# M's stage of a fused attention and expert kernel, issued behind the experts with conversions between its pieces

## The chip, the cores and the metric

The kernel runs on one core of one Trainium2 chip. The metric is the device time of one execution in microseconds (us), the median of several runs. Engines are called TensorE (PE in the profile), VectorE (DVE), ScalarE (ACT), GpSimd (POOL) and SyncE (SP, which issues the DMAs).

## What is computed

Three parts follow one another. Block-causal attention over 8 batches, 8 heads, 576 positions of 64; a soft mixture of 8 experts with 4 slots each over the 4608 tokens of 512; and a last layer of 2048 hidden units whose activation is `s * relu(h)^2 + b`.

```python
def _moe_ref(x, phi, w1, w2):
    ...
    slot_input = d.T @ x
    ...
    for e in range(E):
        h = np.maximum(slot_input[e] @ w1[e], 0.0)
        slot_out[e] = h @ w2[e]
    slot_out = slot_out.reshape(n_slots, D)
    c = logits - logits.max(1, keepdims=True)
    c = np.exp(c)
    c /= c.sum(1, keepdims=True) + 1e-09
    return (c @ slot_out).astype(np.float32)

def _moe2_ref(x, w_in, w_out, s, b):
    h = x @ w_in
    r = np.maximum(h, 0.0)
    g = s * (r * r) + b
    return (g @ w_out).astype(np.float32)
```

`w_in` and `w_out` arrive as 64-bit floats, viewed as pairs of 32-bit integers.

## The kernel before, in words

Attention and routing take the first 430 us and are not touched. Then come three stages.

**Experts (lines 801 to 866).** The weights arrive in 32 pieces of 1 MB: sixteen `w1`, then sixteen `w2`. TensorE works them off with `expert1` and `expert2`, the second layer's sum growing in the PSUM tile `so`. Between the two layers stands `mid`, with ScalarE's copy `hs`. After each piece one call of `convert` issues the next step of the conversions, of which two (`CMOST`) are under way at any time.

**Conversions (`from_f64`, lines 611 to 631, `split_wo` and `conv_in`).** The 16 pieces of `w_in` (`wi`, 8) and `w_out` (`wo`, 8) are put together from the halves of the 64-bit floats: on VectorE L619, L620, L625, L627, on ScalarE L622, L623, a product L706 or L745 on VectorE. A `wo` piece then goes on: ScalarE sums its absolute values (`power`, L710, into `wsum`), VectorE and ScalarE make a power of two of each sum (`power2`, L715, L717, `wpow`), ScalarE writes the high half in 16 bits (`high`, L725, tile `wo_0s` for pieces 0 and 1, `wo_2s` for 2 and 3, and so on) and VectorE the low half (`low`, L730). Each step of a piece is a `yield`, and one call of `convert` takes one step of each active piece. The order of the instructions on each engine is that of the calls in the program. What the expert loop has not issued, the loop of L865 issues behind it.

**M's stage (lines 885 to 976).** M is the product of the expert outputs with w_in: 32 slots by 2048 columns. `slot_rows` copies the sum `so` to `sos` (L894), adds its four row groups on TensorE (L897) and copies that to `soT`. `ctrans` transposes the combine weights of the first group (`ct`). `slots(i)`, eight pieces of 256 columns, makes a product (`m`), a copy `part`, a second product with `J4` (`n`), a sum of absolute values (L914, into `msum`) and a copy into `mf`. Two scales follow: that of M from `msum` (L931 to L939), and that of the output from the maxima of the transposed `mf` (L951 to L975). Each has a product on TensorE that spreads a maximum over all partitions, `gp`. `parts` writes M's high part on ScalarE (L942) and its low part, in rows 64 to 127, on VectorE (L943), in `mst`: first 512 columns, at the end the other 1536.

**Output blocks (lines 980 to 1051).** Twelve groups of three token tiles by 16 blocks of 128 hidden units, 192 blocks. A block is `stage_h` (a product `h`, ScalarE's `r`), `stage_g` (VectorE's `g`), `stage_r` (ScalarE's `rh`, VectorE's `rl`) and `stage_o` (nine products `o` of 512 columns with the halves `hl[f]` of w_out), which is issued `LAG` = 4 blocks behind its `h`. `at(t, ...)` collects these calls with a time number, and they are issued in that order.

Of the kernel before, what the change touches and what calls it, by code (L numbers as in the profile page):

```python
# [40 lines left out]
def fused_kernel(  # L41
# [615 lines left out]
    P = {}  # L657
# [6 lines left out]
    ready, todo, active = set(), [], []  # L664

    toload = list(wseq[NPRE:])
    home = {wseq[i]: wpre[i] for i in range(NPRE)}
# [33 lines left out]
    def split_wo(i):  # L701
# [99 lines left out]
    with tc.manual_schedule():  # L801
# [55 lines left out]
        for kind, i in [x for x in wseq if x[0] in ("w1", "w2")]:  # L857
# [27 lines left out]
    with tc.manual_schedule():  # L885

        pm = ph3.enter_context(tc.tile_pool(name="pm", bufs=3, space=PSUM, reuse_waits="tile"))
        mdone = set()
# [29 lines left out]
        msum = e1.tile([128, 12], F32, name="msum")  # L918
        sb_abs = e1.tile([128, 2], F32, name="sb_abs")
        ACT.activation(out=sb_abs[:, 0:1], in_=s_sb, func=AF.Abs)  # L920
        ACT.activation(out=sb_abs[:, 1:2], in_=b_sb, func=AF.Abs)
# [9 lines left out]
        DVE.tensor_reduce(out=msum[:, 8:9], in_=msum[:, 0:8], axis=AX, op=ALU.add)  # L931
        gp = pm.tile([128, 512], F32, tag="n", name="n")
        PE.matmul(gp[:, 0:128], msum[:, 8:9].to_broadcast([128, 128]), idF, start=True, stop=True)
        DVE.tensor_reduce(out=msum[:, 9:10], in_=gp[:, 0:128], axis=AX, op=ALU.max)
        for n, x in ((10, 0x7F800000), (11, 0)):
            DVE.tensor_scalar(out=msum[:, n:n + 1].bitcast(I32), in0=msum[:, 9:10].bitcast(I32), scalar1=0x7F800000, scalar2=x,
                              op0=ALU.bitwise_and, op1=ALU.bitwise_xor)
        ACT.mul(msum[:, 10:11], msum[:, 10:11], 2.0 ** 13)
        ACT.mul(msum[:, 11:12], msum[:, 11:12], 2.0 ** -28)  # L939

        def parts(x0, x1):
            ACT.activation(out=mst[:, x0:x1], in_=mf[:, x0:x1], func=AF.Copy, scale=msum[:, 10:11])  # L942
            DVE.scalar_tensor_tensor(out=mst[64:128, x0:x1], in0=mf[64:128, x0:x1], scalar=msum[64:128, 10:11],  # L943
                                     in1=mst[64:128, x0:x1], op0=ALU.mult, op1=ALU.subtract)
            mdone.update(range(x0 // 256, x1 // 256))

        parts(0, 512)


        mt = pm.tile([128, 512], F32, tag="m", name="m")  # L950
        for f in range(16):  # L951
            PE.transpose(mt[:, 32 * f:32 * f + 32], mf[0:32, 128 * f:128 * f + 128], idF[0:32, 0:32])

        def small(name, n=16):
            return e1.tile([128, n], F32, name=name)

        mm, bound, gpow, sk, bk, rs_, mu = (small(n) for n in ("mmax", "bound", "gpow", "sk", "bk", "rscale", "mu"))
        DVE.tensor_reduce(out=mm, in_=mt.rearrange("p (f n) -> p f n", n=32), axis=AX, op=ALU.max)
# [12 lines left out]
        DVE.tensor_scalar(out=sk, in0=rs_, scalar1=s_sb, scalar2=1.0, op0=ALU.mult, op1=ALU.mult)
        DVE.tensor_scalar(out=bk, in0=rs_, scalar1=b_sb, scalar2=1.0, op0=ALU.mult, op1=ALU.mult)
        DVE.tensor_scalar(out=mu[:, 3:4].bitcast(I32), in0=mu[:, 1:2].bitcast(I32), scalar1=0x7F800000, scalar2=None,
                          op0=ALU.bitwise_and)
        DVE.tensor_scalar(out=mu[:, 3:4], in0=mu[:, 3:4], scalar1=2.0 ** -28, scalar2=None, op0=ALU.mult)  # L975
        parts(512, 2048)
    ph3.close()
    ps_h = ctx.enter_context(tc.tile_pool(name="ps_h", bufs=2, space=PSUM, reuse_waits="tile"))
    ps_o = ctx.enter_context(tc.tile_pool(name="ps_o", bufs=2, space=PSUM, reuse_waits="tile"))
    with tc.manual_schedule():  # L980
        rr_ = {}

        def stage_h(g, f):
            assert f // 2 in mdone
# [33 lines left out]
        def stage_e(g):  # L1018
            for i in range(3):
                ob = e3.tile([128, 512], F32, tag="ob", name="ob")  # L1020
                if i == 1:
                    DVE.tensor_scalar(out=ob, in0=ops[g][i], scalar1=mu[:, 3:4], scalar2=1.0, op0=ALU.mult, op1=ALU.mult)
                else:
                    ACT.activation(out=ob, in_=ops[g][i], func=AF.Copy, scale=mu[:, 3:4])
# [10 lines left out]
        def step(gen):  # L1035
            next(gen, None)

        for i in range(1, 6):
            for j in range(4):
                at(16 * (2 * i - 1) - 5 + 2 * j + 0.3, step, combs[i])  # L1040
        for n, (g, f) in enumerate(seq):
# [39 lines left out]
```

## Time and profile before

| | |
|---|---|
| median of 3 runs | 983.55 us (982.73 to 985.5) |
| profiled execution | 982.77 us |
| its span in the trace | 981.1 us |
| TensorE products | 879.0 us busy (90%) |
| VectorE | 703.6 us (72%) |
| ScalarE | 604.1 us (62%) |
| GpSimd | 286.5 us (29%) |
| data moved | 91.73 MB, 94 GB/s over the span |

Busy shares are means over stages with different limits. What the change touches lies between about 430 and 590 us of the span, so the rows further down are taken there. In a timeline, the bracket behind a row is the engine's idle time before it and what ended that; a count such as x8 for four products in 32 bits counts two passes of each.

### The profile page before, as it was taken

The page shows a single profiled execution, that of the slowest core. Times are in us where ns is not written, and L with a number is a line of the kernel's source. Part 1 is how long each engine was busy: PE and PEld are TensorE (multiplying, and loading weights), DVE is VectorE, ACT ScalarE, POOL GpSimd, SP SyncE. Part 2 cuts the span into 40 slices and gives each one's busy share as a digit, 9 for nine tenths or more (in the row PEclk, how much of TensorE's full clock was granted, in tenths as well). Part 3 has the DMA queues.
Part 4 walks back from the last instruction along what each step waited for, and adds up shares of the span by engine and source line. Part 5 has one row for each costly group of instructions (what it writes and reads, how often), then busy time and mean ns, then how long its engine had stood idle before and what let it go on. Part 6 is the DMA issues. An engine that isn't in the chain of part 4 may idle for free.

```text
span 981.1 us, 20487 instructions
## 1 busy us (share of the span) xinstructions
PE 879.0 (90%) x8052; PEld 515.1 (53%) x8052; DVE 703.6 (72%) x1269; ACT 604.1 (62%) x1040; POOL 286.5 (29%) x224
## 2 busy tenths in 40 slices
PE   3899989988999988876785699999999999999998
PEld 2677767767777767761110334444444444444443
DVE  5798979888899879848889566565555565565553
ACT  2677767777677767753377655555555555565553
POOL 6576756665566646652000000000000000000000
PEclk9999999999999999987999789999999999999999
DMA  4544544444434434075995000001000100010001
GB/s 113 130 91 118 129 109 101 102 120 115 110 81 123 123 106 112 15 302 217 410 400 214 1 1 33 11 23 33 33 1 32 33 32 2 33 33 1 33 33 32
DMA packets 150927, 91.73 MB, mean 94 GB/s; under 512 B 127472, under 2 KB 127792, under 8 KB 150832
## 3 DMA queue, kind: packets, MB, share of 16 engines
q1 hardware_dynamic: 150832, 90.44, 30.7%
q8 instruction: 63, 1.03, 0.4%
q14 instruction: 32, 0.26, 0.1%
HBM read 80.81 MB, written 9.44 MB: 92 GB/s over the span
## 4 chain that ended last, share of the span: by engine, by line
PE 58%; DVE 21%; ACT 11%; DMA 4%; issue 3%; POOL 3%; SPq 0%; DVEq 0%; POOLq 0%; ACTq 0%
PE o L1015 13%; PE o L1014 13%; PE o L1016 13%; DVE vl L356 5%; PE s L378 4%; DVE mm L292 4%; ACT pc L383 4%; PE h L986 3%; ACT ph L255 3%; PE tp L268 2%; DMA w<-in_moe_w_dram 2%; PE s L303 2%; DVE me L292 2%; PE pv L416 1%; DVE kql L262 1%
## 5 line engine op out<-in xcount | busy, mean ns | idle before, releaser
L262 POOL TENSOR_TENSOR pl<-pc,ph 128x896 f16<-128x896 f32 (+1 forms) x128 | 232.4, 1817 | 150.0 <-ACT ph L255 82.6
L994 DVE SCALAR_TENSOR_TENSOR g<-r,sk 128x384 f32<-128x384 f32 x192 | 119.4, 622 | 128.2 <-ACT r L988 126.7
L988 ACT ACTIVATE r<-h,msum 128x384 f32<-128x384 f32 x192 | 111.4, 581 | 156.4 <-PE h L986 155.3
L383 ACT ACTIVATE pc<-s 128x896 f32<-128x896 f32 (+1 forms) x128 | 110.6, 864 | 75.1 <-PE s L378 48.0
L1002 DVE SCALAR_TENSOR_TENSOR rl<-g,bk,rh 128x384 f16<-128x384 f32 x192 | 117.9, 614 | 8.0 <-ACT rh L1000 6.7
L1000 ACT ACTIVATE rh<-g,bk 128x384 f16<-128x384 f32 x192 | 116.5, 607 | 2.2 <-DVE g L994 2.2
L255 ACT CAST ph<-pc 128x896 f16<-128x896 f32 (+1 forms) x128 | 113.4, 886 | 4.1
L292 DVE TENSOR_REDUCE mm<-s 128x2 f32<-128x1024 f32 (+3 forms) x128 | 101.8, 817 | 7.3 <-PE s L303 7.1
L766 POOL TENSOR_TENSOR c<-lgs,mc 128x192 f32<-128x192 f32 x6 | 3.0, 508 | 345.6 <-DVE mc L764 345.6
L416 PE MATMUL pv<-vh,ph 128*128 128x65 f16 x960 | 102.5, 196 | 1.2 <-DVE xt L432 1.0
L418 PE MATMUL pv<-vh,pl 128*128 128x65 f16 x960 | 101.0, 194 | 1.3 <-POOL pl L262 1.3
L417 PE MATMUL pv<-vl,ph 128*128 128x64 f16 x960 | 101.4, 193 | 0.0
L416 PEld LDWEIGHTS <-ph 128*128 128x128 f16 x960 | 86.6, 98 | 23.0 <-issue 6.3
L1016 PEld LDWEIGHTS <-rl 128*128 128x128 f16 x576 | 56.4, 98 | 68.7 <-DVE rl L1002 0.7
L1014 PEld LDWEIGHTS <-rh 128*128 128x128 f16 x576 | 56.5, 98 | 66.6 <-issue 0.3
L418 PEld LDWEIGHTS <-pl 128*128 128x128 f16 x960 | 88.7, 98 | 1.6 <-POOL pl L262 1.5
L417 PEld LDWEIGHTS <-ph 128*128 128x128 f16 x960 | 88.6, 99 | 0.0
L1015 PEld LDWEIGHTS <-rh 128*128 128x128 f16 x576 | 56.5, 98 | 58.3 <-issue 0.6
L262 DVE TENSOR_TENSOR kql<-tp,kq 128x512 fp32r<-128x512 f32 (+1 forms) x96 | 57.5, 599 | 29.2 <-ACT kq L284 28.2
L268 PE MATMUL tp<-idF,rqk 128*128 128x128 f32 x320 | 57.9, 298 | 22.0 <-DVE kql L262 9.6
L303 PE MATMUL s<-kq 64*128 64x64 f32 (+4 forms) x384 | 55.3, 336 | 20.6 <-DVE me L292 14.6
L378 PE MATMUL s<-kq 64*128 64x128 f32 (+3 forms) x384 | 70.4, 363 | 0.8
(236 smaller groups left out, 1967.7 us busy)
## 6 DMA issues: line engine op xcount, KB each, us to landing
w<-in_moe_w_dram SPq DMA_DIRECT2D x44, 512.0 KB
w2h<-in_moe_w_dram SPq DMA_DIRECT2D x20, 512.0 KB
rqk<-in_k_dram SPq DMA_DIRECT2D x64, 128.0 KB
rqk<-in_q_dram SPq DMA_DIRECT2D x64, 128.0 KB
rv<-in_v_dram SPq DMA_DIRECT2D x64, 128.0 KB
wi<-in_moe_w_in_dram SPq DMA_DIRECT2D x8, 1024.0 KB
wo<-in_moe_w_out_dram SPq DMA_DIRECT2D x8, 1024.0 KB
out_dram<-ob SPq DMA_DIRECT2D x32, 256.0 KB
```

The lines of the kernel that those rows point to most:

```text
L255: ACT.copy(o, i)
L262: eng.tensor_tensor(out=o, in0=i, in1=h, op=ALU.subtract)
L292: DVE.tensor_reduce(out=o, in_=i, axis=AX, op=ALU.max)
L383: ACT.activation(out=pc[:, :, 0:w], in_=st.pop(("ps", p, c))[:, :, 0:w], func=AF.Exp, scale=scale)
L416: PE.matmul(o, a, vh[:, 2 * sl + h, 0:65], start=(c == 0 and n == 0), stop=False)
L417: PE.matmul(o[:, 0:64], a, vl[:, 2 * sl + h, :], start=False, stop=False)
L418: PE.matmul(o, l, vh[:, 2 * sl + h, 0:65], start=False, stop=(c == 3 and n == len(UNIT[c]) - 1))
L994: DVE.scalar_tensor_tensor(out=g0, in0=r, scalar=sk[:, f:f + 1], in1=r, op0=ALU.mult, op1=ALU.mult)
L1002: DVE.scalar_tensor_tensor(out=rl, in0=g0, scalar=bk[:, f:f + 1], in1=rh, op0=ALU.add, op1=ALU.subtract)
L1014: PE.matmul(o, rh[:, 128 * i:128 * i + 128], hl[f][0], start=(f == 0), stop=False)
L1015: PE.matmul(o, rh[:, 128 * i:128 * i + 128], hl[f][1], start=False, stop=False)
L1016: PE.matmul(o, rl[:, 128 * i:128 * i + 128], hl[f][0], start=False, stop=(f == 15))
```

## The change

- The second loop of conversions behind the experts is gone. `slots` yields twice, and the loop over it calls `convert` after each of its first ten rounds, then until all eight `power2` are issued (`summed`). What remains of the conversions is called in the first eight output blocks. The pool of the conversions' tiles outlives the experts for that.
- The sum of absolute values of M (L914, `msum`) is replaced. Each slot's columns of `mf` are transposed (into `mt`, in a bank of its own) as soon as they are copied; `extremes` takes maxima and minima of these, and both scales come from one round: one tile `top` of two columns, two products `gp`, one reduction, and the powers `inv`, `fm`, `fo`.
- All copies `part` and the copy `soT` are ScalarE's, the copies `mf` VectorE's but for the last.
- M's high and low parts are separate calls. Before the output blocks stand 512 columns of the high and 256 of the low part; the others are issued in blocks 0 to 11.
- The lag between `h` and `o` begins at 2 blocks and grows to 4 over the first eight.

```diff
     P["cs"] = later(ctx, "csp", 1).tile([128, NT, 64], F16, name="cs")
     e2 = later(ctx, "e2", 2)
-    P["cv"] = later(ph2, "cv", 2)
+    P["cv"] = later(ctx, "cv", 2)
...
             ACT.mul(wpow[:, 2 * i:2 * i + 2], wpow[:, 2 * i:2 * i + 2], 2.0 ** 13)
+
+            summed.add(i)
...
             convert(CMOST)
-        while todo or active:
-            convert(CMOST)
     ph2.close()
...
-            DVE.tensor_copy(soT, sop[:, 0:128].rearrange("p (c n) -> p c n", c=4))
+            ACT.copy(soT, sop[:, 0:128].rearrange("p (c n) -> p c n", c=4))
...
-            (DVE.tensor_copy if i % 2 else ACT.copy)(part, ps)
+            ACT.copy(part, ps)
             yield
             ps = pm.tile([128, 512], F32, tag="n", name="n")[:, 0:256]
             PE.matmul(ps, J4.rearrange("p a n -> p (a n)"), part, start=True, stop=True)
-
-            ACT.activation(out=part, in_=ps, func=AF.Abs, bias=eps, accum_out=msum[:, i:i + 1])
-            (ACT.copy if i % 2 else DVE.tensor_copy)(mf[:, 256 * i:256 * (i + 1)], ps)
+            (DVE.tensor_copy if i < 7 else ACT.copy)(mf[:, 256 * i:256 * (i + 1)], ps)
+            yield
+            for f in (2 * i, 2 * i + 1):
+                PE.transpose(mt[:, 32 * f:32 * f + 32], mf[0:32, 128 * f:128 * f + 128], idF[0:32, 0:32])
...
+        def extremes(f0, f1):
+
+            x = mt[:, 32 * f0:32 * f1].rearrange("p (f n) -> p f n", n=32)
+            DVE.tensor_reduce(out=mm[:, f0:f1], in_=x, axis=AX, op=ALU.max)
+            DVE.tensor_reduce(out=mn[:, f0:f1], in_=x, axis=AX, op=ALU.min)
+
         gens = [slots(i) for i in range(8)]
-        for i in range(10):
-            if i < 8:
-                next(gens[i])
-            if i >= 2:
-                next(gens[i - 2], None)
...
+        for i in range(11):
+            for j in (i, i - 2, i - 3):
+                if 0 <= j < 8:
+                    next(gens[j], None)
+            if i < 10:
+                convert(CMOST)
+        while len(summed) < 8:
+            convert(CMOST)
...
+        extremes(0, 16)
+
+
+        DVE.scalar_tensor_tensor(out=mn, in0=mn, scalar=-1.0, in1=mm, op0=ALU.mult, op1=ALU.max)
+        DVE.tensor_reduce(out=top[:, 0:1], in_=mn, axis=AX, op=ALU.max)
...
+        DVE.tensor_reduce(out=top[:, 1:2], in_=bound, axis=AX, op=ALU.max)
         gp = pm.tile([128, 512], F32, tag="n", name="n")
-        PE.matmul(gp[:, 0:128], mu[:, 0:1].to_broadcast([128, 128]), idF, start=True, stop=True)
...
+        for n in range(2):
+            PE.matmul(gp[:, 128 * n:128 * n + 128], top[:, n:n + 1].to_broadcast([128, 128]), idF, start=True, stop=True)
+        DVE.tensor_reduce(out=top, in_=gp[:, 0:256].rearrange("p (a n) -> p a n", a=2), axis=AX, op=ALU.max)
...
+        part_hi(0, 256)
...
+        part_lo(0, 256)
...
+        part_hi(256, 512)
...
+        at(0.9, part_lo, 256, 512)
+        for x in range(512, 2048, 512):
+            at(x / 128 - 2.6, part_hi, x, x + 512)
+            at(x / 128 - 1.8, part_lo, x, x + 256)
+            at(x / 128 - 0.8, part_lo, x + 256, x + 512)
+
+        for n in range(8):
+            at(n + 1.3, convert, CMOST)
...
-            at(n + LAG + .05, stage_o, g, f)
+            lag = min(LAG, 2 + n / 4) + .05
+            at(n + lag, stage_o, g, f)
```

Line numbers of the changed kernel lie a few higher: `high` is L727 there (L725 before), `low` L732, the copy `sos` L895, `soT` L899, `part` L910, `mf` L914, M's high part L971, `r` L997, `rh` L1009.

**ScalarE around the end of the experts.** In the order of the kernel before, behind the sums (L710), the powers (L717) and the high part (L725) of piece wo_2; the rows of two such rounds, down to the copy `sos`:

```order
L725 ACTIVATE wo_2s<-cvf,wpow 128x512 x2
L710 ACTIVATE cve,wsum<-cvf,eps 128x512 x2
L717 ACTIVATE wpow<-wpow 128x2
L725 ACTIVATE wo_2s<-cvf,wpow 128x512 x2
L622 ACTIVATE cvf<-wo_8667 128x1024
L623 ACTIVATE cve<-cve,m_103 128x1024
...
L717 ACTIVATE wpow<-wpow 128x2
L725 ACTIVATE wo_6s<-cvf,wpow 128x512 x2
L894 COPY sos<-so 128x512
L710 ACTIVATE cve,wsum<-cvf,eps 128x512 x2
```

and in the changed kernel, from the same high part of wo_2 (here L727):

```order
L727 ACTIVATE wo_2s<-cvf,wpow 128x512 x2
L895 COPY sos<-so 128x512
L899 COPY soT<-m 128x128
L641 COPY ct<-n 64x384
L910 COPY part<-m 128x256
L710 ACTIVATE cve,wsum<-cvf,eps 128x512 x2
L910 COPY part<-m 128x256
L717 ACTIVATE wpow<-wpow 128x2
L910 COPY part<-m 128x256
L727 ACTIVATE wo_2s<-cvf,wpow 128x512 x2
L622 ACTIVATE cvf<-wo_8667 128x1024
```

Before, `sos` stood behind the high part of wo_6 (the last but one of the eight pieces); now it stands behind that of wo_2, and the sums of wo_3 and all later conversions are behind it.

**VectorE at the same place in the changed kernel**, behind the last product (L706) of piece wo_3:

```order
L706 TENSOR_TENSOR cvf<-cvf,cve 128x1024
L642 COPY ct<-n 64x384
L732 SCALAR_TENSOR_TENSOR wo_2s<-cvf,wpow,wo_2s 128x512 x2
L715 TENSOR_SCALAR wpow<-wsum 128x2
L914 COPY mf<-n 128x256
L619 TENSOR_SCALAR cve<-wo_8667 128x1024
L620 TENSOR_SCALAR cvm<-wo_8667 128x1024
L914 COPY mf<-n 128x256
L732 SCALAR_TENSOR_TENSOR wo_2s<-cvf,wpow,wo_2s 128x512 x2
L625 SCALAR_TENSOR_TENSOR cvf<-cvm,cvf 128x1024
L914 COPY mf<-n 128x256
```

The copy `ct` stood behind the last `wpow` before; it now comes ahead of the low part of wo_2, and the copies `mf` alternate with conversions of wo_3 to wo_5.

**ScalarE from the last power to the first output blocks in the changed kernel:**

```order
L717 ACTIVATE wpow<-wpow 128x2
L971 ACTIVATE mst<-mf,fm 128x256 x2
L997 ACTIVATE r<-h,fo 128x384 x2
L727 ACTIVATE wo_6s<-cvf,wpow 128x512 x2
L971 ACTIVATE mst<-mf,fm 128x512
L1009 ACTIVATE rh<-g_9490,bk 128x384
L997 ACTIVATE r<-h,fo 128x384
```

The high part of wo_7 (in the tile `wo_6s`), which stood ahead of M's stage, now comes between the first two `r` and the first `rh`, together with the next 512 columns of M's high part.

## Rows read from the trace of the kernel before

**Rows 1.** Stretches: us, busy time of each engine, granted clock, DMA share, GB/s.

```profile
458.50:531.40 72.90, 57.97 (x234) 9.24 (x234) 62.16 (x75) 40.31 (x62) 0.00 (x0) 1.00 0.99 386
531.40:543.20 11.80, 0.00 (x0) 0.00 (x0) 10.54 (x15) 9.05 (x17) 0.00 (x0) 0.68 0.00 0
...
585.75:981.10 395.35, 390.58 (x1867) 180.58 (x1864) 224.73 (x402) 217.33 (x405) 8.29 (x14) 1.00 0.07 25
```

**Rows 2.** TensorE timeline: start, length, engine, line, op, names, shapes, count, idle before.

```profile
530.30 1.05 PE L853 MATMUL so<-w,hTz 128*32 128x512 f32 x4 [0.25 <-DMA w<-in_moe_w_dram]
543.80 1.92 PE L897 MATMUL m<-I,sos 128*128 128x32 f32 x8 [12.46 <-ACT sos L894]
...
567.33 0.63 PE L1014 MATMUL o<-wo_0s,rh 128*128 128x512 f16 x1
...
585.75 0.38 PE L1014 MATMUL o<-wo_4s,rh 128*128 128x512 f16 x1
```

**Rows 3.** ScalarE timeline, same columns: conversions and the copy of the expert sums.

```profile
514.28 1.33 ACT L725 ACTIVATE wo_2s<-cvf,wpow 128x512 f16<-128x512 f32 x2
516.43 0.72 ACT L710 ACTIVATE cve<-cvf,eps 128x512 f32<-128x512 f32 x1 [0.82 <-DVE cvf L706]
...
543.19 0.56 ACT L894 COPY sos<-so 128x512 f32<-128x512 f32 x1
```

**Rows 4.** VectorE timeline: the last power of w_out and what stood before it.

```profile
545.76 0.29 DVE L898 COPY soT<-m 128x128 f32<-128x128 f32 x1 [0.37 <-PE m L897]
545.97 0.16 DVE L715 TENSOR_SCALAR wpow<-wsum 128x2 int32<-128x2 int32 x1
```

**Rows 5.** ScalarE and VectorE timelines, 485 to 494 us: the wait at `hs`.

```profile
489.67 0.69 ACT L839 ACTIVATE hs<-hp,rs 128x512 f32<-128x512 f32 x1 [7.08 <-PE hp L825]
...
493.16 1.23 DVE L625 SCALAR_TENSOR_TENSOR cvf<-cvm,cvf 128x1024 f32<-128x1024 int32 x1 [6.35 <-ACT cvf L622]
```

**Rows 6.** A stretch of that wait, columns as in rows 1.

```profile
488.00:490.00 2.00, 1.31 (x7) 0.15 (x6) 0.00 (x0) 0.33 (x1) 0.00 (x0) 1.00 1.05 385
```

**Rows 7.** Stretches for the clock, columns as in rows 1.

```profile
534.00:536.00 2.00, 0.00 (x0) 0.00 (x0) 1.86 (x3) 2.00 (x3) 0.00 (x0) 0.90 0.00 0
...
549.00:550.00 1.00, 1.00 (x10) 0.47 (x10) 0.33 (x1) 0.59 (x2) 0.00 (x0) 0.88 0.00 0
```

**Rows 8.** The chain that ended last: start, length, engine, tile, line, count.

```profile
549.71 0.57 PE m L905 x8
```

**Rows 9.** VectorE timeline: two copies of the M stage, one behind the other.

```profile
550.40 0.42 DVE L915 COPY mf<-n 128x256 f32<-128x256 f32 x1 [1.07 <-issue]
550.74 0.41 DVE L909 COPY part<-m 128x256 f32<-128x256 f32 x1
```

**Rows 10.** The stretch of the remaining conversions, columns as in rows 1.

```profile
516.43:546.13 29.70, 14.34 (x62) 3.67 (x59) 26.76 (x36) 22.55 (x41) 0.00 (x0) 0.82 0.41 158
```

**Rows 11.** VectorE and TensorE timelines: the chain of the scales.

```profile
560.55 0.69 DVE L958 TENSOR_REDUCE mmax<-m 128x16 f32<-128x512 f32 x1
...
563.16 0.29 DVE L966 TENSOR_REDUCE mu<-n 128x1 f32<-128x128 f32 x1 [0.89 <-PE n L965]
...
563.86 0.23 DVE L970 TENSOR_SCALAR rscale<-gpow,mu 128x16 f32<-128x16 f32 x1
...
562.33 0.80 PE L965 MATMUL n<-idF,mu 128*128 128x128 f32 x2 [2.99 <-DVE mu L963]
```

**Rows 12.** Lines L942 and L943: count, ns shortest/median/longest, starts.

```profile
L942 ACT ACTIVATE mst<-mf,msum x2: 722/1140/1559, 559.0 to 559.6; 128x512 f16<-128x512 f32 x1, 128x1536 f16<-128x1536 f32 x1
...
L943 DVE SCALAR_TENSOR_TENSOR mst<-mf,msum,mst x2: 752/1286/1819, 559.8 to 565.2; 64x512 f16<-64x512 f32 x1, 64x1536 f16<-64x1536 f32 x1
```

**Rows 13.** The page, costliest groups: busy, mean ns, idle before and its releaser.

```profile
L988 ACT ACTIVATE r<-h,msum 128x384 f32<-128x384 f32 x192 | 111.4, 581 | 156.4 <-PE h L986 155.3
...
L1000 ACT ACTIVATE rh<-g,bk 128x384 f16<-128x384 f32 x192 | 116.5, 607 | 2.2 <-DVE g L994 2.2
```

**Rows 14.** TensorE timeline: the first output product at its later length.

```profile
569.81 0.38 PE L1014 MATMUL o<-wo_0s,rh 128*128 128x512 f16 x1
```

More of the change, by code (lines that the diff above doesn't have):

```diff
@@ L661, in fused_kernel @@
     e2 = later(ctx, "e2", 2)
-    P["cv"] = later(ph2, "cv", 2)
+    P["cv"] = later(ctx, "cv", 2)
     wpost = places(ph2, "wpost", NPOST, reuse_waits="tile")
-    ready, todo, active = set(), [], []
+    ready, summed, todo, active = set(), set(), [], []
     toload = list(wseq[NPRE:])
@@ L917, in fused_kernel, with small @@
         mf = mstp.tile([128, 2048], F32, name="mf")
-        msum = e1.tile([128, 12], F32, name="msum")
         sb_abs = e1.tile([128, 2], F32, name="sb_abs")
-        ACT.activation(out=sb_abs[:, 0:1], in_=s_sb, func=AF.Abs)
-        ACT.activation(out=sb_abs[:, 1:2], in_=b_sb, func=AF.Abs)
+        def small(name, n=16):
+            return e1.tile([128, n], F32, name=name)
+        mm, mn, bound, gpow, sk, bk, rs_ = (small(n) for n in ("mmax", "mmin", "bound", "gpow", "sk", "bk", "rscale"))
@@ L922, in fused_kernel @@
+        top, power, inv, fm, fo = (small(n, 2) for n in ("top", "power", "inv", "fm", "fo"))
         slot_rows()
         ctrans(0, pm, "n")
-        gens = [slots(i) for i in range(8)]
-        for i in range(10):
-            if i < 8:
-                next(gens[i])
-            if i >= 2:
-                next(gens[i - 2], None)
-        DVE.tensor_reduce(out=msum[:, 8:9], in_=msum[:, 0:8], axis=AX, op=ALU.add)
-        gp = pm.tile([128, 512], F32, tag="n", name="n")
-        PE.matmul(gp[:, 0:128], msum[:, 8:9].to_broadcast([128, 128]), idF, start=True, stop=True)
@@ L934, in fused_kernel @@
[L934 to L958, printed above, removed]
+        mt = pmt.tile([128, 512], F32, name="mt")
@@ new lines, in fused_kernel @@
+        while len(summed) < 8:
+            convert(CMOST)
+        for n, c in enumerate((s_sb, b_sb)):
+            DVE.tensor_scalar(out=sb_abs[:, n:n + 1].bitcast(I32), in0=c.bitcast(I32), scalar1=0x7FFFFFFF, scalar2=None,
+                              op0=ALU.bitwise_and)
+        DVE.tensor_scalar(out=gpow.bitcast(I32), in0=wsum.bitcast(I32), scalar1=0x7F800000, scalar2=None, op0=ALU.bitwise_and)
+        extremes(0, 16)
+        DVE.scalar_tensor_tensor(out=mn, in0=mn, scalar=-1.0, in1=mm, op0=ALU.mult, op1=ALU.max)
@@ L970, in fused_kernel @@
-        DVE.tensor_scalar(out=rs_, in0=gpow, scalar1=mu[:, 2:3], scalar2=2.0 ** 13, op0=ALU.mult, op1=ALU.mult)
+        for n in range(2):
+            PE.matmul(gp[:, 128 * n:128 * n + 128], top[:, n:n + 1].to_broadcast([128, 128]), idF, start=True, stop=True)
+        DVE.tensor_reduce(out=top, in_=gp[:, 0:256].rearrange("p (a n) -> p a n", a=2), axis=AX, op=ALU.max)
+        DVE.tensor_scalar(out=top, in0=top, scalar1=2.0 ** -60, scalar2=None, op0=ALU.max)
+        DVE.tensor_scalar(out=inv.bitcast(I32), in0=top.bitcast(I32), scalar1=0x7F800000, scalar2=0x7F800000,
+                          op0=ALU.bitwise_and, op1=ALU.bitwise_xor)
@@ new lines, in fused_kernel, with part_hi, part_lo @@
+        DVE.tensor_scalar(out=fm, in0=inv, scalar1=2.0 ** 13, scalar2=None, op0=ALU.mult)
+        def part_hi(x0, x1):
+            ACT.activation(out=mst[:, x0:x1], in_=mf[:, x0:x1], func=AF.Copy, scale=fm[:, 0:1])
+        def part_lo(x0, x1):
+            DVE.scalar_tensor_tensor(out=mst[64:128, x0:x1], in0=mf[64:128, x0:x1], scalar=fm[64:128, 0:1],
+                                     in1=mst[64:128, x0:x1], op0=ALU.mult, op1=ALU.subtract)
+            mdone.update(range(x0 // 128, x1 // 128))
@@ L971, in fused_kernel @@
+        part_hi(0, 256)
+        DVE.tensor_scalar(out=power.bitcast(I32), in0=top.bitcast(I32), scalar1=0x7F800000, scalar2=None, op0=ALU.bitwise_and)
+        DVE.tensor_scalar(out=fo, in0=power, scalar1=2.0 ** -28, scalar2=None, op0=ALU.mult)
+        DVE.tensor_scalar(out=rs_, in0=gpow, scalar1=inv[:, 1:2], scalar2=2.0 ** 13, op0=ALU.mult, op1=ALU.mult)
+        part_lo(0, 256)
         DVE.tensor_scalar(out=sk, in0=rs_, scalar1=s_sb, scalar2=1.0, op0=ALU.mult, op1=ALU.mult)
         DVE.tensor_scalar(out=bk, in0=rs_, scalar1=b_sb, scalar2=1.0, op0=ALU.mult, op1=ALU.mult)
-        DVE.tensor_scalar(out=mu[:, 3:4].bitcast(I32), in0=mu[:, 1:2].bitcast(I32), scalar1=0x7F800000, scalar2=None,
-                          op0=ALU.bitwise_and)
@@ L987, in stage_h @@
             r = e3.tile([128, 384], F32, tag="r", name="r")
-            ACT.activation(out=r, in_=hps, func=AF.Relu, scale=msum[:, 11:12])
+            ACT.activation(out=r, in_=hps, func=AF.Relu, scale=fo[:, 0:1])
             rr_[g, f] = r
@@ L1021, in stage_e @@
                 if i == 1:
[L1022 removed]
+                    DVE.tensor_scalar(out=ob, in0=ops[g][i], scalar1=fo[:, 1:2], scalar2=1.0, op0=ALU.mult, op1=ALU.mult)
                 else:
[L1024 removed]
+                    ACT.activation(out=ob, in_=ops[g][i], func=AF.Copy, scale=fo[:, 1:2])
                 for p0, p1, r0 in tok_rows(3 * g + i):
@@ L1046, in fused_kernel @@
             at(n + T["r"], stage_r, g, f)
-            at(n + LAG + .05, stage_o, g, f)
+            lag = min(LAG, 2 + n / 4) + .05
+            at(n + lag, stage_o, g, f)
             if f == 15:
-                at(n + LAG + .06, stage_e, g)
+                at(n + lag + .01, stage_e, g)
         for t, _, fn, args in sorted(ops_at, key=lambda x: x[:2]):
```

10 lines of the change are left out of this document (2 added, 8 removed).

## The prediction

> **What bounds the kernel now.** I read the stretches first. Up to 531.4 us TensorE works on the experts' products and the DMA engines are 99% busy: the loads of the expert weights set the pace. From 585.75 us to the end TensorE is busy for 390.58 of 395.35 us: the output blocks set it. In 531.4 to 543.2 TensorE does nothing at all [rows 1], and the product that then opens the M stage had waited 12.46 us for ScalarE's copy `sos` [rows 2]. Meanwhile VectorE and ScalarE convert w_out in turn. So up to 585.75 us the question is only when the output blocks can begin; behind that every block takes 2.1 us on TensorE (395 us for 184 blocks and a tail) in both kernels, and a shift at 585.75 comes out whole at the end.
>
> The timelines give the marks. The last expert product ends at 530.30 + 1.05 = 531.35, the first output product starts at 567.33, and block 8 (the first to read `wo_4s`) at 585.75 [rows 2]. ScalarE finished the high part of wo_2 at 514.28 + 1.33 = 515.61, began the sums of wo_3 at 516.43, and copied `sos` only at 543.19 [rows 3]: all the time between it was converting. VectorE's last power (`wpow` of wo_7) ended at 545.97 + 0.16 = 546.13 [rows 4].
>
> **The change, part by part.** *Where the copy now stands.* The order shows `sos` on ScalarE straight behind the high part of wo_2, and all sums, powers and high parts of wo_3 to wo_7 behind it. ScalarE works its queue in order, and `sos` reads what the last expert product writes. So ScalarE comes to the copy at 515.61 and stands until 531.35: 15.7 us in which it converted before. VectorE stands too, at the copy `ct`, which needs the M stage's transposes. The kernel before has the same thing once: the copy `hs` waits 7.08 us for the first half of the experts, and VectorE idles 6.35 us for the conversion that is queued on ScalarE behind it [rows 5]. The loads went on at 385 GB/s in that stop [rows 6], and the order has the same loads. So 531.35 stands.
>
> *From there to the first conversion.* `sos` 0.56 [rows 3]; four products 1.0 (half of the 1.92 at the lower clock [rows 2]; TensorE kept the full one for some 4 us after the experts, 0.90 being granted in 534 to 536 [rows 7]); the copy `soT`, now ScalarE's, 0.3 (0.29 on VectorE [rows 4]); a slot's four products 0.57 [rows 8]; its copy `part` 0.3; five hand-overs of 0.03. That is 2.9 us, and 4.5 at the lower clock. The sums of wo_3 start at 534.3 and not at 516.43: 17.9 us late.
>
> *The conversions that remain.* From 516.43 to 546.13 they took 29.7 us, with 0.37 in a wait for `soT` that is gone [rows 4]: 29.3. Put between them are seven copies `mf` on VectorE, 0.34 each from start to start [rows 9], and on ScalarE seven more `part` and one `mf`, about as long: 2.4 and 2.7 us. They cost nothing if all fall into waits, and 5.1 if none does. Of the 29.7 us VectorE is busy 26.76 and ScalarE 22.55 [rows 10]. VectorE is the fuller one, so I take most of its own copies and none of ScalarE's: 2.1. The last power ends at 534.3 + 29.3 + 2.1 = 565.7; it ended at 546.1.
>
> *From the last power to the first output product.* Before: 567.33 - 546.13 = 21.2 us. Slots, transposes and their copies are done by now, and the separate pass for the sum of absolute values is gone. What is left: three short ones 0.3; the maxima and the new minima 1.35 (0.69 each); six short ones 1.2 (five took 561.24 to 562.33); the two products of the common round 1.1 (0.80 for one); their maxima and three short ones 0.95 (0.70 before, for half the width) [rows 11]; the high part of 256 columns 0.47 and its late part 0.42 (each between half and all of the 0.72 and 0.75 for 512 [rows 12]); `h` 0.45 (between an output product's 0.38 and 0.63 [rows 2]); two `r` 1.1; then on ScalarE, which the order puts ahead of the first `rh`, the high part of wo_7 1.3 [rows 3] and 512 columns of M 0.65; `rh` 0.6 [rows 13]. With 0.2 for hand-overs this is 10.1; bounds 8 and 12, by a fifth either way on so many short pieces. The first output product starts at 575.8.
>
> *The first blocks.* From block 0 to block 8 it was 18.4 us. The lag now starts at 2 and grows to 4, so ten `h` lie between these marks and not eight: eight blocks at 2.1 make 16.8, two more `h` 0.3 (2.1 over nine products of 512 columns and one of 384). On top come the low part of wo_7 on VectorE, 1.4, ahead of block 1's late part, and the lower clock: TensorE made its first six output products in 567.33 to 569.81, 0.41 from start to start and not 0.21 [rows 2, 14]; nine such cost 1.8. The two overlap in part, and I take 1.9 (1.0 to 3.2): 19.0. M's remaining parts in blocks 1 to 10 are hidden by TensorE's 2.1 us a block, in which VectorE and ScalarE have two operations of some 0.6 each [rows 13]; without that cover each would cost its 0.4 or 0.65.
>
> *The sum.* Block 8 starts at 575.8 + 19.0 = 594.8 and not at 585.75: 9.1 us later. The profiled execution took 982.77, so 991.9. It lies 0.8 below the median of the runs shown, within their own spread; I forecast **992.0 us**. The bounds: 1.6 more at the start, 2.1 less or 3.0 more for the copies, 2 either way for the scales, 0.9 less or 1.3 more for the blocks. Since they will not all fall to one side, the forecast's own range is 988.5 to 996.
>
> **The rivals.** *The interleaving pays* (faster). The M stage lies beside conversions that lose no time by it. Then the last power ends at 546.1 - 0.4 + 2.1 = 547.9, the first output product starts 10.1 later, and block 8 at 577.0: 8.8 us earlier, 974.0 us. For it: TensorE's 12.46 us of waiting are there to be won [rows 2], and ScalarE has idle time [rows 10]. Against it: this needs the expert sum by the time ScalarE comes to the copy, 515.61. It decides where the delay of 17.9 falls below 8.8, that is a sum done by 522.3; but the last expert product still waited on a load at 530 [rows 2]. The Trainium skill ("Perfetto Trace Analysis", section Optimization Strategy) says that regimes with different most-contended engines may run better when interleaved; by that rule it would be these 974.0 us. The trace speaks against it here: what is queued ahead of the copy was beside the experts already, and what is behind it loses that place. Chance 0.06.
>
> *A colder TensorE* (slower still). Between about 551 and 571 us TensorE has little to do. After its idle stretch to 543.8 it came back to the full clock only in 549 to 550 (0.88 granted [rows 7]), some five us after it had work again. Should three of the first blocks run at half speed, at 1.9 each, of which one is counted: 995.7 and more. Against it: the clock rose 2.5 us after the first output product [rows 14]. Chance 0.09.
>
> *The copies are free* and the first blocks lose nothing: 2.1 + 1.9 less, 988 us. Chance 0.06.
>
> *No net change*: this needs all low bounds together and the conversions catching up besides. VectorE alone has 26.76 us of work in the 29.7 [rows 10]. Chance 0.03.
>
> **How the numbers follow.** The forecast has 0.76. A measurement of this kernel can tell about 0.3%, 3 us, from no change. Slower by more: forecast, colder TensorE and free copies, 0.91. Within: 0.03. Faster: 0.06. The range 988 to 996.5 leaves out the faster rival, no change, and most of the colder one.
>
> **What would show it.** ScalarE's `sos` copy should carry an idle time of some 15.7 us, ended by TensorE's product of `so`, and start at about 531.4. TensorE's gap behind the experts should shrink from 12.46 us to 0.6. The last `wpow` should stand near 565.7, the first output product near 575.8, block 8 near 594.8, with 395 us behind it. Should the copy carry no such idle time, or the last `wpow` lie before 555, the argument is wrong at its root.

## The result, and the profile after

The changed kernel takes 993.63 us (median of 6 runs, 991.99 to 997.01). In the same comparison the kernel before takes 983.84 us (median of 6). The ratio is 1.0097 with a 95% interval of 1.0081 to 1.0113: slower by about 1%. The profiled execution took 994.55 us with a span of 992.8, 0.9 above the median of its runs; that of before lay 1.1 below its own.

ScalarE's timeline of the changed kernel, to be held against [rows 3]:

```profile
516.63 1.33 ACT L727 ACTIVATE wo_2s<-cvf,wpow 128x512 f16<-128x512 f32 x2
534.30 0.58 ACT L895 COPY sos<-so 128x512 f32<-128x512 f32 x1 [16.34 <-PE so L855]
536.05 0.27 ACT L899 COPY soT<-m 128x128 f32<-128x128 f32 x1 [1.17 <-PE m L898]
...
537.35 0.72 ACT L710 ACTIVATE cve<-cvf,eps 128x512 f32<-128x512 f32 x1
...
572.87 0.91 ACT L971 ACTIVATE mst<-mf,fm 128x256 f16<-128x256 f32 x2 [4.35 <-DVE fm L968]
...
575.43 1.33 ACT L727 ACTIVATE wo_6s<-cvf,wpow 128x512 f16<-128x512 f32 x2
576.66 0.71 ACT L971 ACTIVATE mst<-mf,fm 128x512 f16<-128x512 f32 x1
577.27 0.61 ACT L1009 ACTIVATE rh<-g,bk 128x384 f16<-128x384 f32 x1
```

Behind the high part of wo_2, ScalarE stands for 16.34 us until TensorE's last product `so` is there. In the kernel before, the sums of wo_3 (L710) followed that high part after 0.8 us (515.61 to 516.43); now they follow after 19.4 (517.96 to 537.35), which is 18.6 us later.

VectorE's timeline of the changed kernel:

```profile
517.52 1.23 DVE L706 TENSOR_TENSOR cvf<-cvf,cve 128x1024 f32<-128x1024 f32 x1
536.84 0.35 DVE L642 COPY ct<-n 64x384 f16<-64x384 f16 x1 [18.10 <-ACT ct L641]
537.21 1.41 DVE L732 SCALAR_TENSOR_TENSOR wo_2s<-cvf,wpow,wo_2s 128x512 f16<-128x512 f32 x2
...
568.11 0.17 DVE L715 TENSOR_SCALAR wpow<-wsum 128x2 int32<-128x2 int32 x1 [0.26 <-ACT cve L710]
```

VectorE stands for 18.10 us at the copy `ct`, with the low part of wo_2, which could have run, queued behind it. By the order this low part (1.41 us) is all that VectorE's own stop holds up: the operation behind it is the power of wo_3, and that needs the sums which stand behind `sos` on ScalarE. The last power ends at 568.28; it ended at 546.13 before [rows 4].

TensorE's timeline of the changed kernel, to be held against [rows 2]:

```profile
533.20 1.05 PE L855 MATMUL so<-w,hTz 128*32 128x512 f32 x4 [0.27 <-DMA w<-in_moe_w_dram]
534.94 1.08 PE L898 MATMUL m<-I,sos 128*128 128x32 f32 x8 [0.69 <-ACT sos L895]
...
570.14 1.62 PE L962 MATMUL n<-idF,top 128*128 128x128 f32 x4 [17.68 <-DVE top L955]
...
577.93 0.61 PE L1023 MATMUL o<-wo_0s,rh 128*128 128x512 f16 x1 [1.01 <-ACT rh L1009]
578.33 0.63 PE L1024 MATMUL o<-wo_0s,rh 128*128 128x512 f16 x1
...
581.32 0.63 PE L1025 MATMUL o<-wo_0s,rl 128*128 128x512 f16 x1
...
597.55 0.38 PE L1023 MATMUL o<-wo_4s,rh 128*128 128x512 f16 x1
```

The gap behind the experts has shrunk from 12.46 us to 0.69, as the change says. But a gap of 17.68 us stands in front of the scales instead: M's slots are done, and TensorE waits for the conversions. Block 8 starts at 597.55; 395.25 us lie behind it (span 992.8), and 395.35 did before.

The stretches of the changed kernel (us, busy time of PE, PEld, DVE, ACT, POOL, granted clock, DMA share, GB/s), to be held against [rows 1]:

```profile
461.00:534.25 73.25, 57.99 (x234) 9.24 (x234) 48.85 (x59) 29.10 (x42) 0.00 (x0) 1.00 0.99 386
534.25:577.90 43.65, 16.39 (x115) 8.00 (x114) 35.44 (x67) 30.12 (x62) 0.00 (x0) 0.70 0.00 0
```

While the expert weights arrive, ScalarE is now busy for 29.10 us and VectorE for 48.85, where it was 40.31 and 62.16 in a stretch of the same length: about 11 and 13 us of conversions left the cover of the loads. The loads themselves did not change (386 GB/s, share 0.99).

Marks of two executions are compared below by their distance from the experts' end (in this trace 533.20 + 1.05 = 534.25, before 531.35), because that end itself lies up to 3.4 us apart in these ten traces; the last section shows it. From the experts' end to block 8 it took 54.40 us before and takes 63.30 now: 8.9 more.

### The profile page after: what moved, and what is told of

It is laid out like the page before. It is cut to its first block, busy times and chain, and to the rows that moved or that the text cites. A ratio compares the mean times of both kernels' runs of the same rounds, so it can differ in the third digit from the quotient of the medians.

```text
span 992.8 us, 20483 instructions
## 1 busy us (share of the span) xinstructions
PE 883.4 (89%) x8052; PEld 517.0 (52%) x8052; DVE 705.1 (71%) x1275; ACT 599.9 (60%) x1025; POOL 286.9 (29%) x224
## 4 chain that ended last, share of the span: by engine, by line
PE 57%; DVE 19%; ACT 9%; DMA 9%; issue 3%; POOL 2%; SPq 0%; DVEq 0%; POOLq 0%; ACTq 0%
PE o L1023 13%; PE o L1024 13%; PE o L1025 13%; PE s L378 5%; DVE vl L356 4%; DMA w<-in_moe_w_dram 4%; DVE mm L292 3%; ACT pc L383 3%; PE h L995 3%; DMA w2h<-in_moe_w_dram 3%; PE tp L268 2%; ACT ph L255 2%; PE s L303 2%; DMA mr<-mT 2%; PE pv L416 1%
## 5 line engine op out<-in xcount | busy, mean ns | idle before, releaser
L997 ACT ACTIVATE r<-h,fo 128x384 f32<-128x384 f32 x192 | 111.1, 579 | 156.1 <-PE h L995 154.9
L1009 ACT ACTIVATE rh<-g,bk 128x384 f16<-128x384 f32 x192 | 116.2, 605 | 0.2 <-DVE g L1003 0.2
L378 PE MATMUL s<-mr,neg 64*128 64x128 f32 (+3 forms) x384 | 67.5, 321 | 7.0 <-DMA mr<-mT 6.5
```

## The experiments

The theory: the loss is the stop of ScalarE at `sos` (and of VectorE at `ct`), for it puts some 16 us of conversions behind the experts. The rivals: the loss lies in the new round of scales, in the split parts or in the shorter lag; or the interleaving itself costs. A run is called by the first two characters of its name. Each ratio is to the kernel before in the same comparison; the changed kernel, e1 to e4, e5 to e7 and e8 stand in four of them, and between these the ratios are to be set beside each other and not the times. "Last power", "first product" and "block 8" are times from the experts' end of the same trace.

| kernel | ratio to before [95%] | wait at `sos` | last power | first product | block 8 |
|---|---|---|---|---|---|
| before | | none | 14.78 | 35.98 | 54.40 |
| after | 1.0097 [1.0081, 1.0113] | 16.34 | 34.03 | 43.68 | 63.30 |
| e3_move_only | 1.0122 [1.0105, 1.0139] | 16.10 | 36.28 | 48.89 | 67.43 |
| e2_ahead_all | 0.9998 [0.9986, 1.001] | none | 14.35 | 35.23 | 55.41 |
| e4_ahead4 | 1.0039 [1.0023, 1.0055] | 9.85 | 28.02 | 37.67 | 56.97 |
| e1_ahead10 | 0.9927 [0.9905, 0.995] | none | 18.29 | 28.40 | 48.83 |
| e8_ahead14 | 0.9937 [0.992, 0.9954] | none | 17.56 | 30.02 | 48.94 |
| e5_rh_first | 0.9915 [0.9901, 0.9929] | none | 18.32 | 27.21 | 46.93 |
| e6_lag4 | 0.9937 [0.9923, 0.995] | none | 18.12 | 29.76 | 48.97 |
| e7_warm | 0.9931 [0.9918, 0.9945] | none | 18.12 | 29.47 | 48.16 |

**The move alone, in the kernel before** (e3_move_only): the two old passes of scales, the old copies, the old parts and the lag of 4 stay.

```diff
-    P["cv"] = later(ph2, "cv", 2)
+    P["cv"] = later(ctx, "cv", 2)
...
-        while todo or active:
-            convert(CMOST)
...
             if i >= 2:
                 next(gens[i - 2], None)
+            convert(CMOST)
+        while todo or active:
+            convert(CMOST)
```

> The kernel before with the move alone: M's stage straight behind the experts, one call of the conversions after each of its ten rounds and the rest ahead of the scales; both old scale rounds, old parts, lag 4. Theory: ScalarE stands 15 to 17 us at sos, the first output product comes near 578, ratio 1.009 to 1.013. Rival (the loss is in the new scales, parts or lag): ratio 0.995 to 1.0.

Measured: 997.24 us, ratio 1.0122 [1.0105, 1.0139]. ScalarE's timeline of this kernel:

```profile
515.40 1.33 ACT L725 ACTIVATE wo_2s<-cvf,wpow 128x512 f16<-128x512 f32 x2
532.84 0.59 ACT L892 COPY sos<-so 128x512 f32<-128x512 f32 x1 [16.10 <-PE so L853]
```

The move alone has the whole loss and the same wait. Block 8 comes 67.43 us after the experts, 13.0 later than before and 4.1 later than in the changed kernel. So the loss needs nothing of the rest of the change. That the rest even lessens it rests on the marks of two traces, since the intervals of the two ratios overlap; and part of the 4.1 is that here all conversions stand ahead of the scales, while the changed kernel leaves the last steps of wo_7 to the output blocks. (The first product was expected near 578 us and came at 581.68.)

**The rest without the move** (e2_ahead_all): the changed kernel with the loop behind the experts put back.

```diff
             convert(CMOST)
+        while todo or active:
+            convert(CMOST)
     ph2.close()
```

> The changed kernel with all conversions issued ahead of M's stage, as before the change; the scale round, the late parts and the short first lag stay. The copy sos then stands on ScalarE where it stood before. Theory: the rest of the change is worth little by itself, minus 0.5 to minus 3 us, ratio 0.997 to 1.0; first output product near 565 to 567. Rival (the loss is in the scale round, the late parts or the lag): ratio 1.005 to 1.01.

Measured: 985.55 us, ratio 0.9998 [0.9986, 1.001]; `sos` waits for nothing and the last power comes 14.35 us after the experts, about as before (14.78). The scales, the parts and the lag cost nothing in sum that the medians show; the gain of 0.5 to 3 us that was expected is not seen either. ScalarE's timeline of this kernel:

```profile
543.50 0.56 ACT L897 COPY sos<-so 128x512 f32<-128x512 f32 x1
```

VectorE's timeline shows what the slots cost when no conversion stands between them:

```profile
553.61 0.42 DVE L916 COPY mf<-n 128x256 f32<-128x256 f32 x1 [1.01 <-PE n L915]
555.05 0.42 DVE L916 COPY mf<-n 128x256 f32<-128x256 f32 x1 [1.01 <-PE n L915]
```

A slot takes 1.44 us, and VectorE idles for 1.01 of it. From the last power to the first product it is 20.88 us here (21.2 before), and from there to block 8 20.18 (18.42 before). That sum is 1.4 us longer than before; the medians do not show it (interval from 0.14% less to 0.1% more). It lies in the first eight blocks: they begin with twelve products of more than 0.45 us where it was six before (an output product takes 0.63 us at the low clock and 0.38 at the full one), and hold two more `h`.

**Four calls of `convert` ahead of the copy** (e4_ahead4) and **ten** (e1_ahead10): half the wait removed, and all of it.

```diff
             convert(CMOST)
+        for _ in range(4):
+            convert(CMOST)
     ph2.close()
```

> The changed kernel with four more calls of the conversions ahead of M's stage: ScalarE comes to sos behind the high part of wo_3, some 6 us of conversions later. Theory: the idle time before sos shrinks from 16 to 9 or 10 us, and the total by the same 5 to 7 us: ratio 1.002 to 1.006. Rival (the wait at sos is not what costs): no change from the 1.0097 of the change.

> The changed kernel with ten more calls of the conversions between the experts and M's stage, so that ScalarE comes to the copy sos behind the sums of wo_5, at about the time the experts end. Theory (ScalarE's queue stands at the copy, and the conversions behind it are lost time): no idle time of more than 2 us before sos; last wpow near 548, first output product near 558 to 560, block 8 near 578 to 580; 976 to 978 us, ratio to the kernel before 0.991 to 0.995, faster than both. Rival (the loss comes from the new scale round, the late parts and the short lag, wherever the copy stands): ratio 1.005 to 1.01, as the change. Rival (M's pieces between conversions hold them up by as much as the wait): ratio 1.00 or above.

Measured: with four calls 988.24 us, ratio 1.0039 [1.0023, 1.0055]; with ten 978.91 us, 0.9927 [0.9905, 0.995], faster than both kernels. ScalarE's timeline with four:

```profile
533.88 0.59 ACT L897 COPY sos<-so 128x512 f32<-128x512 f32 x1 [9.85 <-PE so L855]
```

and with ten:

```profile
531.28 0.72 ACT L710 ACTIVATE cve<-cvf,eps 128x512 f32<-128x512 f32 x1 [0.84 <-DVE cvf L706]
...
532.70 0.56 ACT L897 COPY sos<-so 128x512 f32<-128x512 f32 x1
534.43 0.27 ACT L901 COPY soT<-m 128x128 f32<-128x128 f32 x1 [1.17 <-PE m L900]
...
535.46 0.37 ACT L912 COPY part<-m 128x256 f32<-128x256 f32 x1 [0.27 <-PE m L908]
```

VectorE's and TensorE's timelines with ten, the last power and block 8:

```profile
550.58 0.17 DVE L715 TENSOR_SCALAR wpow<-wsum 128x2 int32<-128x2 int32 x1
```

```profile
581.29 0.38 PE L1025 MATMUL o<-wo_4s,rh 128*128 128x512 f16 x1
```

With ten, ScalarE comes to `sos` 0.24 us after the experts' end (531.41 + 1.05 = 532.46) and does not stand at it. The wait goes 16.34, 9.85, 0, and block 8 goes 63.30, 56.97, 48.83. The first 6.49 us of wait taken away gave 6.33 us, the other 9.85 gave 8.14. At the last power the two steps gave 6.01 and 9.73; most of what the second lacks at block 8 is lost in the first blocks, which begin with thirteen products at the low clock's length with ten calls and with nine with four. The size of the loss follows the size of the wait, and the theory stands. The rivals of the scales, the parts and the lag fall with e2 and e3; that the interleaving itself costs falls with e1, which keeps M's slots between the conversions. (Its last power was expected near 548 us and came at 550.75, block 8 at 578 to 580 and came at 581.29; 1.1 of that is the later experts' end of this trace.)

**Fourteen calls** (e8_ahead14), to see whether more is better:

```diff
-        for _ in range(10):
+        for _ in range(14):
```

> As the run with ten rounds behind the experts, but fourteen. The question is whether the ten rounds that just use up the wait at the copy sos are the right number, or whether more is better or indifferent. Theory (what costs time is only that ScalarE stands at sos): ten rounds already leave no wait, so four more bring nothing; sos starts some 5 to 6 us after the experts' last product, TensorE stands as long, the last wpow comes at about the same time after the experts (17 to 18.5 us; it was 18.29 with ten rounds and 14.35 with all), but the last slots now come after fewer conversions and stand more alone: block 8 lies 0 to 3 us later than with ten rounds, ratio 0.993 to 0.996. Rival (every conversion ahead of M's stage is a gain, the bound being the last wpow): wpow 2 us earlier and block 8 too, ratio 0.991 or less. Second rival (M's stage bounds as soon as sos is late): block 8 is 5 us later than with ten rounds, ratio 0.998.

Measured: 979.42 us, ratio 0.9937 [0.992, 0.9954], not to be told from ten. ScalarE's and TensorE's timelines of this kernel:

```profile
538.81 0.57 ACT L897 COPY sos<-so 128x512 f32<-128x512 f32 x1
```

```profile
533.66 1.05 PE L855 MATMUL so<-w,hTz 128*32 128x512 f32 x4 [0.27 <-DMA w<-in_moe_w_dram]
539.43 1.91 PE L900 MATMUL m<-I,sos 128*128 128x32 f32 x8 [4.71 <-ACT sos L897]
```

TensorE now waits 4.71 us for `sos` (the copy came 4.1 us after the experts; 5 to 6 were expected), and its four products take 1.91 us and not 1.08 (the granted clock is 0.50 in 538 to 540). The maxima at the head of the scales wait for M's last slot, in both kernels; with ten calls and with fourteen, on VectorE:

```profile
551.31 0.69 DVE L937 TENSOR_REDUCE mmax<-mt 128x16 f32<-128x512 f32 x1 [0.36 <-PE mt L919]
```

```profile
556.39 0.69 DVE L937 TENSOR_REDUCE mmax<-mt 128x16 f32<-128x512 f32 x1 [0.32 <-PE mt L919]
```

From the experts' end that is 18.85 and 21.68 us. So with ten calls the slots and the conversions already end almost together, and with fourteen the slots end later: the maxima lose 2.8 us. The first product is only 1.6 later, for the high part of wo_7 (1.3) is done ahead of M's scales here, and block 8 lies at 48.94, 0.1 later than with ten, for the eight blocks take 18.92 us and not 20.43, with seven products at the low clock's length and not thirteen. TensorE's wait is not free, then; it was made up behind it.

**The first `rh` ahead of what is not needed yet** (e5_rh_first): ten calls, and in the output's first blocks the high part of wo_7 and M's next 512 columns come behind the first `rh` and not ahead of it.

```diff
-            at(x / 128 - 2.6, part_hi, x, x + 512)
+            at(max(x / 128 - 2.6, 1.7), part_hi, x, x + 512)
...
-            at(n + 1.3, convert, CMOST)
+            at(n + 1.75, convert, CMOST)
```

> e1_ahead10 with the first rh issued ahead of the high part of wo_7 and of M's next 512 columns on ScalarE. Theory (these two stood in the path to the first output product, 1.33 and 0.71 us): the first output product comes 1.5 to 2 us earlier after the last wpow, 8 us instead of 10.3; the total 0.5 to 2 us below e1, ratio to the kernel before 0.990 to 0.993. Rival (the late parts are then late for h3 and h4, TensorE waits there instead): the same as e1.

Measured: 976.48 us, ratio 0.9915 [0.9901, 0.9929], the fastest of all. ScalarE's timeline:

```profile
556.64 1.05 ACT L999 ACTIVATE r<-h,fo 128x384 f32<-128x384 f32 x2 [0.71 <-PE h L997]
557.96 0.61 ACT L1011 ACTIVATE rh<-g,bk 128x384 f16<-128x384 f32 x1 [0.27 <-DVE g L1005]
558.48 0.71 ACT L973 ACTIVATE mst<-mf,fm 128x512 f16<-128x512 f32 x1
559.09 1.32 ACT L727 ACTIVATE wo_6s<-cvf,wpow 128x512 f16<-128x512 f32 x2
```

From the last power to the first product it is 8.89 us against 10.11 with ten calls alone: 1.2 us (1.5 to 2 were expected) for some 2.0 us of ScalarE's work put behind. Part comes back as a wait of `rh` for `g` (0.27). Block 8 comes 1.9 earlier; the other 0.7 are gained in the blocks, which begin with ten products at the low clock's length and not thirteen. The intervals of the two kernels overlap, so that this edit by itself is worth something rests on the marks of two traces and not on the medians.

**A lag of 4 throughout** (e6_lag4): ten calls, and the lag of the kernel before.

```diff
-            lag = min(LAG, 2 + n / 4) + .05
+            lag = LAG + .05
```

> e1_ahead10 with the lag of 4 blocks from the first block on. Theory (the short first lag lets the output products start two blocks of ScalarE's work earlier): first output product 2 to 3 us later, two h fewer between it and block 8, total 1 to 2.5 us above e1. Rival (the short lag gives nothing, since the first blocks wait for the late parts and run at the lower clock anyway): within 0.5 us of e1.

Measured: 978.71 us, ratio 0.9937 [0.9923, 0.995], the same as with the short lag, as the rival said; 1 to 2.5 us more were expected. The first product comes 1.4 us later (29.76), and the eight blocks behind it take 19.21 us and not 20.43; at block 8 0.1 us is left. The two `h` that no longer lie between these marks are 0.3 of the 1.2 (0.16 each); most of the rest is the clock, nine products at the low clock's length and not thirteen. Whether the lag or this one execution made the clock rise sooner is not shown.

**A busier TensorE ahead of the output** (e7_warm): ten calls, and four added products, two behind the last power and two behind the products `gp`.

```diff
+        def busy(n):
+            for _ in range(n):
+                PE.matmul(warm[0:16, :], wpow, mf[:, 0:512], start=True, stop=True)
...
+        busy(2)
...
             PE.matmul(gp[:, 128 * n:128 * n + 128], top[:, n:n + 1].to_broadcast([128, 128]), idF, start=True, stop=True)
+        busy(2)
```

> e1_ahead10 with four added products of 16 by 512 in 32 bits into a bank that nobody reads: two behind the last power of w_out, two behind the products of the common scale round. Theory (TensorE, idle for some 9 us before the scales, makes its first nine output products at the lower clock, 0.43 us each instead of 0.215): with work from the last power on it is granted the full clock before the first output product; 1.5 to 2.5 us less between the last wpow and block 8, ratio 0.989 to 0.992. Rival (the first blocks wait for VectorE and ScalarE, the clock is hidden behind that): within 0.5 us of e1, with the output products at 0.215 and gaps between them. If the added products come in the way of the scale round, up to 1 us more.

Measured: 978.40 us, ratio 0.9931 [0.9918, 0.9945], not to be told from the run without them. The stretches with ten calls alone:

```profile
558.00:560.00 2.00, 0.48 (x1) 0.10 (x1) 1.72 (x3) 2.00 (x5) 0.00 (x0) 0.50 0.00 0
560.00:562.00 2.00, 1.14 (x3) 0.38 (x4) 1.11 (x3) 1.78 (x4) 0.00 (x0) 0.50 0.00 0
...
564.00:566.00 2.00, 2.00 (x7) 0.76 (x5) 1.03 (x3) 0.70 (x2) 0.00 (x0) 0.50 0.00 0
566.00:568.00 2.00, 2.00 (x10) 0.79 (x8) 1.06 (x2) 0.38 (x1) 0.00 (x0) 0.83 0.00 0
```

and with the added products:

```profile
554.00:556.00 2.00, 2.00 (x6) 0.93 (x4) 0.04 (x1) 0.00 (x0) 0.00 (x0) 0.50 0.00 0
556.00:558.00 2.00, 2.00 (x5) 0.38 (x4) 1.51 (x8) 0.75 (x2) 0.00 (x0) 0.68 0.00 0
558.00:560.00 2.00, 0.97 (x4) 0.11 (x2) 1.13 (x4) 1.31 (x4) 0.00 (x0) 1.00 0.00 0
560.00:562.00 2.00, 0.32 (x1) 0.10 (x1) 1.24 (x3) 2.00 (x4) 0.00 (x0) 1.00 0.00 0
...
564.00:566.00 2.00, 1.27 (x7) 0.44 (x6) 1.97 (x5) 1.11 (x2) 0.00 (x0) 1.00 0.00 0
```

The clock did what was wanted: granted at 1.00, the full 2.4 GHz level, when the first output product starts at 562.29, where it is 0.50 (1.2 GHz) until 566 without the added products. But the products stand in TensorE's queue ahead of what the chain of scales needs: the first product comes 1.2 us later after the last power (11.35 against 10.11), and blocks at full clock then wait for their `rl` (TensorE is busy for 1.27 of the 2 us from 564 to 566). From there to block 8 it is 18.69 and not 20.43. From the last power to block 8 that is 0.5 us less, where 1.5 to 2.5 were expected; at block 8 0.7 us is left, inside the spread.

## Why the prediction was right

The direction, the mechanism and the size came out by the steps of the forecast; each term stands beside its measurement.

| term | forecast, us | measured, us |
|---|---|---|
| ScalarE's wait at `sos` (from before's 515.61 to the experts' end) | 15.7 | 16.34 |
| experts' end to the first conversion | 2.9 | 3.1 (537.35 - 534.25) |
| first conversion to the last power's end | 31.4 (29.3 + 2.1) | 30.9 (568.28 - 537.35) |
| last power to the first output product | 10.1 | 9.65 (577.93 - 568.28) |
| first product to block 8 | 19.0 | 19.6 (597.55 - 577.93) |
| experts' end to block 8, against before | +9.1 | +8.9 (63.30 - 54.40) |

- *Where the copy stands.* Read from the order, and carried by the precedent of `hs` [rows 5]: an engine that works its queue in order, a copy that reads a later result, and work behind it that could have run. It came as said, on both engines. e3 shows that it alone suffices, and e2 that the rest of the change loses nothing that its interval shows.
- *From the experts' end to the first conversion* the sum was right partly by luck. It left out the copy `ct` (0.47 on ScalarE), which the order puts there, and counted the slot's products whole (0.57), which ran beside that copy and left a wait of 0.27.
- *The copies among the conversions* were between 0 and 5.1 us, taken at 2.1, VectorE being the fuller engine. The sum with the conversions was 0.5 too long, which leaves 1.6 for the copies.
- *The scales and the first blocks* were 0.45 too long and 0.6 too short; the two nearly cancel. The first nine products, at 0.42 from start to start (577.93 to 581.32), show the low clock that was counted. The rival of a colder TensorE, with three blocks at half speed, did not come.
- *531.35 stands* did not hold in this trace: the experts ended at 534.25. The 2.9 us were there at the end of the attention part already, ahead of everything that the change touches (last section). They are why the profiled time of 994.55 lies 2.7 above the 991.9 that the sum gave: 2.9 from there and 0.2 the other way. The medians differ by 9.8 us, the traces from the experts' end to block 8 by 8.9, which is 0.9%, within the interval of the ratio (0.81% to 1.13%).

**The rival of the other side, "the interleaving pays", had its condition right and its price wrong.** It needed the sum by the time ScalarE comes to the copy, and put the turning point at a delay of 8.8 us, which is a wait of 6.6 (the delay of 17.9 was the wait of 15.7 and 2.2 more). Between e4 (9.85 us of wait, 2.57 later than before at block 8) and e1 (no wait, 5.57 earlier) the straight line crosses zero at 9.85 x 5.57 / 8.14 = 6.7. The line stands on two single traces, and no run lies near its crossing, so that the two numbers agree this closely is partly luck. Where the condition holds the rival was to bring 8.8 us, and e1 brings 5.57. Two terms were too small. The last power comes 3.5 us later than before (18.29 against 14.78) and not 1.7, and VectorE's timeline with ten calls shows the largest wait that was not counted:

```profile
531.16 1.41 DVE L732 SCALAR_TENSOR_TENSOR wo_4s<-cvf,wpow,wo_4s 128x512 f16<-128x512 f32 x2
535.22 0.35 DVE L642 COPY ct<-n 64x384 f16<-64x384 f16 x1 [2.65 <-ACT ct L641]
```

The chain from `sos` over `soT` to `ct` lets VectorE stand for 2.65 us even when `sos` comes in time; the rival had no such term. And the blocks up to block 8 took 20.43 us and not 19.0, more of its products at the low clock (thirteen against the nine that were counted; 566 to 568 us still shows 0.83).

The Trainium skill ("Perfetto Trace Analysis", section Optimization Strategy) says that regimes with different most-contended engines may do better interleaved. e1 agrees with it (0.9927), and the changed kernel does not (1.0097); the two differ in ten calls of `convert`, that is in which work stands ahead of the first instruction that waits for the other regime.

What stays open: the value of e5's edit alone, which the medians do not show, and whether e5 with fewer added products than e7 gains more, which was not tried. In the ten traces the first blocks begin with none to thirteen products at the low clock, each of which costs about 0.21 us, so that small differences of block 8's mark do not rank two of these kernels.

## What to carry to other kernels

When work is interleaved with a stage that has not begun, find on every engine the first instruction that waits for that stage, and ask when its input comes: all that the new order puts behind this instruction loses the cover that it had until then. Place that instruction by the arrival of its input and not by the place of the stage in the program; here ten calls of a generator turn a loss of 1.0% into a gain of 0.7%. A gap of TensorE (12.46 us here) shows who waits, and its length is not the gain: look which queue's end sets the next stage, and keep that queue fed.

## What the runs showed of the hardware

The end of the attention part, which no edit here touches, lies up to 3 us apart in these traces. The last product `pv` of the attention part in the kernel before:

```profile
432.15 0.19 PE L418 MATMUL pv<-vh,pl 128*128 128x65 f16 x1
```

and in the changed kernel:

```profile
435.13 0.19 PE L418 MATMUL pv<-vh,pl 128*128 128x65 f16 x1
```

In the eight other profiles it lies between 432.57 and 434.46. The experts' end follows the start of this product by 98.8 to 99.4 us in nine of the ten, and by 101.0 in the run with fourteen calls; from block 8 to the end of the span it is 395.25 to 395.35 us in all ten. Between two single traces, a shift of 3 us at a mark need not be an effect of an edit, and distances between marks repeat better, if not always. Each trace is one execution of another kernel, so it is not shown whether the kernel or the execution makes the shift; the medians speak for the execution, since they differ by 9.8 us between the two kernels where the two profiled executions differ by 11.8. I had not expected so much from a part whose lines do not differ, and what makes it was not tried.
